# Top-32 threshold of sparse attention: all rows take the search that starts on pairwise larger and smaller halves

## Chip, cores and metric

The kernel runs on one core of a Trainium2 chip. The metric is the device time of one execution in microseconds; the median over several runs counts. The engines are named as in the profile: PE is TensorE, DVE is VectorE, ACT is ScalarE, POOL is GpSimd, SP is SyncE, which here issues most of the transfers.

## The reference

Three layers in a row, all in fp32. The change lies in the first.

```python
scores = scale * np.matmul(q, k.transpose(0, 1, 3, 2))      # 4 x 8 heads, 576 x 576
kth = np.partition(scores, -32, axis=-1)[..., -32:-31]      # the 32nd largest of each row
scores = np.where(scores >= kth, scores, -1e9)
attn = softmax(scores)                                       # exp(scores - max) / sum
x = (attn @ v) reshaped to 2304 x 512
x = ((x @ w_a) * (x @ w_b)) @ w_out                          # 512 -> 1536 -> 512
out = top-1 of 8 experts: gate * (relu(x @ w1[e]) @ w2[e])
```

## The kernel before

The 4 x 8 heads of 576 query rows are cut into 144 tiles of 128 query rows (here called rows of the program). One step of the main loop (line 864) handles one such row on every engine. For row r, PE multiplies and ACT evicts the 128 x 576 scores `s` in two halves (`scores`, lines 364 and 365, two steps ahead). DVE then looks for the 32 largest scores of each query (`topk`, lines 368 to 390) in seven instructions that count: MAX8 writes the eight largest of its input to `t8`, MATCH_REPLACE8 writes the input with these eight set to a very low number, and this repeats until the fourth MAX8 leaves the 32nd largest as its last column. Line 390 turns that into `bi`, a bias for ACT. `softmax` (lines 392 to 402) runs two steps later: ACT makes a penalty for all scores under the threshold (line 397), POOL subtracts it from the scores (line 400, `z<-s,z`), ACT takes the exponential (line 402). PE transposes the result (`turn`, line 419), ACT evicts it (line 422), and `mix` multiplies with v.

Two rows are in work on DVE at a time: lines 904 to 906 take turns between the second half of the row before (`thresholds[0]`) and the first half of the row now (`cur`). The instruction order on PE, DVE, ACT and POOL is fixed by hand; SP's transfers are placed by a scheduler that estimates when they become due. The second layer (lines 639, 652, 683) is fed in pieces into the same steps on PE, ACT and POOL. In the first part of the run weights that come as raw 64-bit words are unpacked as well: two DVE instructions (lines 532 and 534), one on ACT, one on POOL (line 539) and two on PE for each of 36 blocks. The expert layer comes after the attention, from about 880 us on.

`topk` has two forms. The constant FOLD (line 45) is a tuple by which a row picks its form: `FOLD[step % len(FOLD)]` on line 903. With `(0,)` every row takes the plain form: `views = [(t.s, y)] + [(y, y)] * 3`, 576 columns throughout.

Of the kernel before, what the change touches and what calls it, by code (L numbers as in the profile page):

```python
# [41 lines left out]
YB = 2  # L42
XG = 1
RB = 2
FOLD = (0,)
PEN = (0,)
PC = 512
TB = 2
# [34 lines left out]
def fused_kernel(  # L83
# [114 lines left out]
    with ExitStack() as ph:  # L198
# [169 lines left out]
        def topk(t, fold):  # L368


            H2 = S // 2
            t.bi = wk.tile([P, 2], F32, name="bi", bufs=6)
            y = wk.tile([P, S], F32, name="y", bufs=YB)

            t8 = wk.tile([P, 32], F32, name="t8", bufs=6)
            t.top, t.thr = t8[:, 0:1], t8[:, 31:32]
            if fold:
                dve.tensor_tensor(y[:, :H2], t.s[:, :H2], t.s[:, H2:], op=OP.max)
                dve.tensor_tensor(y[:, H2:], t.s[:, :H2], t.s[:, H2:], op=OP.min)
                views = [(y[:, :H2], y[:, :H2])] * 2 + [(y, y)] * 2  # L380
            else:
                views = [(t.s, y)] + [(y, y)] * 3
            for r, (cur, rest) in enumerate(views):
                v = t8[:, r * 8 : r * 8 + 8]
                dve.max(v, cur)  # L385
                yield
                if r < 3:
                    dve.match_replace(out=rest, in_to_replace=v, in_values=cur, imm_value=LOWEST)  # L388
                    yield
            dve.tensor_scalar(t.bi[:, 1:2], t.thr, HUGE, None, op0=OP.mult)  # L390
# [473 lines left out]
        for step in range(-AHEAD_L, NRW + TL + 5):  # L864
# [25 lines left out]
            with tc.high_priority(offset=FG):  # L890
# [11 lines left out]
                if 0 <= step < NRW:  # L902
                    cur = topk(live[step], FOLD[step % len(FOLD)])
                for _ in range(4):
# [404 lines left out]
```

## Time and profile before

| | |
|---|---|
| runs | median 1327.95 us of 3 (1326.23 to 1329.16) |
| profiled execution | 1326.2 us, of which the span from first to last instruction is 1324.5 us |
| PE matmul | 1181.9 us busy, 89% of the span |
| DVE | 913.1 us, 69% |
| ACT | 821.6 us, 62% |
| POOL | 719.9 us, 54% |
| granted TensorE clock, mean | 0.955 |

The shares are averages over unlike stages. Up to about 880 us the 144 rows run and DVE is nearly full; after that DVE has little to do and PE is full. Busy times of one engine do not count overlap of neighbours twice, so a mean duration times a count is a little more than the busy time. A wait is put down to the engine whose signal came last.

### The profile page before, as it was taken

How to read it: one execution, taken by the hardware profiler on the slowest of the kernel's cores; microseconds unless marked ns; L12 is line 12 of the kernel's file. 1: busy time of each engine (PE TensorE's matmuls, PEld its weight loads, DVE VectorE, ACT ScalarE, POOL GpSimd, SP SyncE). 2: the span in 40 equal slices, each digit the busy share in tenths (PEclk: the TensorE clock that was granted, in tenths of full speed). 3: DMA queues.
4: the chain of work that ended last, by engine and by line, in shares of the span. 5: the costliest groups of instructions: out<-in, count | busy, mean ns of one | idle time of the engine just before them, and what ended most of it. 6: DMA issues, size and time to landing. Idle time of an engine off the chain costs nothing. (4 is left out here: it accounts for less than half of the span.)

```text
span 1324.5 us, 23353 instructions
## 1 busy us (share of the span) xinstructions
PE 1181.9 (89%) x7908; PEld 996.1 (75%) x7909; DVE 913.1 (69%) x1995; ACT 821.6 (62%) x1961; POOL 719.9 (54%) x1188
## 2 busy tenths in 40 slices
PE   4766988898999987999998998899999989999996
PEld 3544766677898876888887887677898868888885
DVE  6999999988898986999988898750200135444440
ACT  4777888777777775687777776662532334444441
POOL 4555786766677775767766766564445321111100
PEclk9677999999999997999999998899999989999999
DMA  6334476466695654766765667458988145555520
GB/s 211 118 108 140 159 248 219 164 215 211 202 258 166 187 194 135 209 191 195 194 194 175 204 180 211 135 154 268 324 282 253 32 129 198 174 170 168 177 91 19
DMA packets 129101, 240.56 MB, mean 182 GB/s; under 512 B 24621, under 2 KB 73901, under 8 KB 128978
## 3 DMA queue, kind: packets, MB, share of 16 engines
q1 hardware_dynamic: 124818, 228.74, 55.3%
q0 software_dynamic: 4160, 10.29, 2.4%
q8 instruction: 64, 1.05, 0.3%
q14 instruction: 59, 0.48, 0.1%
HBM read 198.92 MB, written 40.85 MB: 181 GB/s over the span
## 5 line engine op out<-in xcount | busy, mean ns | idle before, releaser
L385 DVE MAX8 t<-y 128x8 f32<-128x576 f32 x432 | 312.0, 750 | 2.9
L400 POOL TENSOR_TENSOR z<-s,z 128x576 f32<-128x576 f32 x144 | 206.0, 1430 | 98.0 <-ACT z L397 95.9
L683 PE MATMUL ab<-xg,wab 128*128 128x256 f32 x1440 | 214.4, 291 | 4.8 <-ACT gab L687 3.1
L388 DVE MATCH_REPLACE8 y<-t,y 128x576 f32<-128x576 f32 x288 | 213.9, 743 | 0.0
L683 PEld LDWEIGHTS ab<-xg,wab 128*128 128x128 f32 x1440 | 189.2, 192 | 8.1 <-ACT gab L687 3.5
L683 PE MATMUL ab<-raw,wab 128*128 128x256 f32 x1152 | 173.4, 292 | 7.2 <-ACT gab L687 4.3
L419 PE MATMUL tr<-ident,z 128*128 128x128 f32 x720 | 137.9, 292 | 41.4 <-ACT z L402 34.7
L683 PEld LDWEIGHTS ab<-raw,wab 128*128 128x128 f32 x1152 | 152.2, 193 | 10.7 <-ACT gab L687 5.0
L402 ACT ACTIVATE z<-z,bi 128x576 f32<-128x576 f32 x144 | 111.4, 774 | 78.2 <-POOL z L400 78.0
L385 DVE MAX8 t<-s 128x8 f32<-128x576 f32 x144 | 107.8, 748 | 59.9 <-ACT s L365 49.0
L364 PE MATMUL tr<-kT,qT 128*128 128x288 f32 x512 | 129.2, 336 | 21.5 <-ACT qT L341 10.9
L422 ACT ACTIVATE wt<-tr 128x384 f32<-128x384 f32 (+2 forms) x320 | 127.3, 412 | 18.5 <-PE tr L419 18.0
L365 ACT ACTIVATE s<-tr 128x288 f32<-128x288 f32 x288 | 118.9, 414 | 30.3 <-PE tr L364 28.7
L652 PE MATMUL x<-wo,gh 128*128 128x512 f32 x432 | 137.7, 400 | 0.0
L419 PEld LDWEIGHTS tr<-ident,z 128*128 128x128 f32 x720 | 92.7, 148 | 56.4 <-ACT z L402 38.8
L1015 DVE TENSOR_TENSOR u<-raw,u 128x1024 fp32r<-128x1024 f32 x64 | 76.3, 1221 | 85.3 <-ACT u L1014 62.5
L639 POOL TENSOR_TENSOR gab<-gab 128x256 f32<-128x256 f32 x108 | 81.5, 754 | 97.0 <-ACT gab L687 92.0
L1064 POOL DMA_INDIRECT out_dram<-o,ids x24 | 23.9, 994 | 201.0 <-ACT o L1063 197.7
L1092 PE MATMUL y<-u,hT 128*128 128x512 f32 (+1 forms) x528 | 128.0, 396 | 0.4 <-DVE hT L1197 0.4
L364 PEld LDWEIGHTS tr<-kT,qT 128*128 128x128 f32 x512 | 90.5, 207 | 37.1 <-ACT qT L341 13.2
L397 ACT ACTIVATE z<-s,bi 128x576 f32<-128x576 f32 x144 | 112.5, 781 | 0.0
L1092 PEld LDWEIGHTS y<-u,hT 128*128 128x128 f32 (+1 forms) x528 | 89.7, 174 | 27.6 <-DVE hT L1197 0.5
(178 smaller groups left out, 2213.8 us busy)
## 6 DMA issues: line engine op xcount, KB each, us to landing
wab<-wab_d SPq DMA_DIRECT2D x192, 512.0 KB, 4.4
raw<-in_moe_w_dram SPq DMA_DIRECT2D x28, 1024.0 KB, 5.1
wab_d<-wab SPq DMA_DIRECT2D x24, 512.0 KB, 3.2
kT<-kT_d SPq DMA_DIRECT2D x20, 576.0 KB, 4.5
vs<-in_v_dram SPq DMA_DIRECT2D x36, 256.0 KB, 3.0
kT_d<-kT SPq DMA_DIRECT2D x16, 576.0 KB, 3.7
raw<-in_moe_w_a_dram SPq DMA_DIRECT2D x12, 512.0 KB, 4.1
raw<-in_moe_w_b_dram SPq DMA_DIRECT2D x12, 512.0 KB, 4.3
```

What stands on the lines that cost most here:

```text
L364: pe.matmul(p, l, r, start=(i == 0), stop=(i == len(terms) - 1))
L365: act.activation(t.s[:, cs], p, AF.Copy, scale=SCALE)
L385: dve.max(v, cur)
L388: dve.match_replace(out=rest, in_to_replace=v, in_values=cur, imm_value=LOWEST)
L397: act.activation(t.w, t.s, AF.Relu, bias=t.bi[:, 1:2], scale=-HUGE)
L400: pool.tensor_tensor(t.w, t.s, t.w, op=OP.subtract)
L402: act.activation(t.w, t.w, AF.Exp, bias=t.bi[:, 0:1], accum_out=t.o.sm[:, t.slot : t.slot + 1])
L419: pe.transpose(pt[:, i * P : (i + 1) * P], t.w[:, k0 : k0 + P], ident)
L422: act.activation(th[:, sl, w], pv[:, :, src], AF.Copy)
L652: pe.matmul(px[t], g[:, ts], wo[:, w, f], start=(f == 0 and i == 0), stop=(f == NF - 1 and i == 2))
L683: pe.matmul(p[:, i], wt[:, a, c, :], xg[x][:, c, :], start=(j == 0), stop=(j == len(terms) - 1))
L1092: pe.matmul(p[:m], (hi, lo)[a], u[:, b, f % 4, :], start=(f == 0 and i == 0), stop=(f == NF2 - 1 and i == 2))
```

## The change

The constant FOLD goes from (0,) to (1,): every row takes the other form of `topk`.

```diff
-FOLD = (0,)
+FOLD = (1,)
```

The lines of `topk` that now run for every row:

```python
dve.tensor_tensor(y[:, :H2], t.s[:, :H2], t.s[:, H2:], op=OP.max)   # H2 = 288
dve.tensor_tensor(y[:, H2:], t.s[:, :H2], t.s[:, H2:], op=OP.min)
views = [(y[:, :H2], y[:, :H2])] * 2 + [(y, y)] * 2
```

Column j of a row is paired with column j + 288; the larger of each pair goes to the left half of `y`, the smaller to the right half. The first 16 largest of the left half are each among the 31 largest of the row, so the first two rounds of MAX8 and MATCH_REPLACE8 search and blank 288 columns only; the last two rounds (MAX8, MATCH_REPLACE8, MAX8) run over all 576. A row has four MAX8 and three MATCH_REPLACE8 as before and two TENSOR_TENSOR more.

On DVE, in the middle of the attention, one step before (number behind `t_` is the row's own buffer; 3952 is the older row, 4011 the newer):

```order
L385 MAX t_3952<-y 128x8
L385 MAX t_4011<-s 128x8
L388 MATCH_REPLACE y<-t_3952,y 128x576
L388 MATCH_REPLACE y<-t_4011,s 128x576
L385 MAX t_3952<-y 128x8
L385 MAX t_4011<-y 128x8
L390 TENSOR_SCALAR bi<-t_3952 128x1
L388 MATCH_REPLACE y<-t_4011,y 128x576
```

And the same step after, where 4050 is the older row and 4111 the newer:

```order
L385 MAX t_4050<-y 128x8
L378 TENSOR_TENSOR y<-s 128x288
L379 TENSOR_TENSOR y<-s 128x288
L385 MAX t_4111<-y 128x8
L388 MATCH_REPLACE y<-t_4050,y 128x576
L388 MATCH_REPLACE y<-t_4111,y 128x288
L385 MAX t_4050<-y 128x8
L385 MAX t_4111<-y 128x8
L390 TENSOR_SCALAR bi<-t_4050 128x1
L388 MATCH_REPLACE y<-t_4111,y 128x288
```

The two TENSOR_TENSOR stand ahead of the newer row's first MAX8, whose place among the others is as it was. The instructions on PE, ACT and POOL and their order are the same in both kernels. On SP three places near the start differ. One of them, a load of k, before:

```order
L241 DMA kr<-in_k_dram 128x2x256
L246 DMA kr<-in_k_dram 64x64 x2
L512 DMA raw_607<-in_moe_w_out_dram 128x1024
L228 DMA qr<-in_q_dram 128x128 x2
L334 DMA kT_d<-kT 128x1152
```

and after:

```order
L241 DMA kr<-in_k_dram 128x2x256
L246 DMA kr<-in_k_dram 64x64
L512 DMA raw_621<-in_moe_w_out_dram 128x1024
L228 DMA qr<-in_q_dram 128x128 x2
L246 DMA kr<-in_k_dram 64x64
L334 DMA kT_d<-kT 128x1152
```

One small load has moved behind three others.

## Rows read from the trace of the kernel before

**Rows 1.** Stages: busy time (and instructions) of each engine, clock, DMA share, GB/s
```profile
33.00:300.00 267.00, 211.59 (x1266) 157.97 (x1265) 249.12 (x541) 209.91 (x476) 174.53 (x231) 0.87 0.52 172
300.00:880.00 580.00, 535.60 (x4040) 460.22 (x4040) 511.79 (x1174) 420.00 (x1110) 398.47 (x706) 0.97 0.64 190
```

**Rows 2.** Instruction groups of DVE, whole span: busy us, mean ns, idle before
```profile
L385 DVE MAX8 t<-y 128x8 f32<-128x576 f32 x432 | 312.0, 750 | 2.9
L388 DVE MATCH_REPLACE8 y<-t,y 128x576 f32<-128x576 f32 x288 | 213.9, 743 | 0.0
...
L1015 DVE TENSOR_TENSOR u<-raw,u 128x1024 fp32r<-128x1024 f32 x64 | 76.3, 1221 | 85.3 <-ACT u L1014 62.5 <-DMA raw<-in_moe_w_dram 22.6
...
L737 DVE MAX8 m<-lg 128x8 f32<-128x8 f32 x18 | 2.9, 163 | 35.1 <-ACT lg L733 35.1
L739 DVE FIND_INDEX8 i<-m,lg 128x8 uint32<-128x8 f32 x18 | 2.9, 160 | 0.0
```

**Rows 3.** Timeline of DVE: start us, us; two MAX8 in a row
```profile
319.41 1.41 DVE L385 MAX8 t<-y 128x8 f32<-128x576 f32 x2
```

**Rows 4.** DVE groups, 33 to 300 us
```profile
L385 DVE MAX8 t<-s 128x8 f32<-128x576 f32 x42 | 31.2, 742 | 4.6 <-ACT s L365 4.6
...
L534 DVE TENSOR_SCALAR w64r<-raw 128x512 int16<-128x512 int16 x33 | 24.6, 745 | 0.0
L532 DVE TENSOR_SCALAR w64t<-raw 128x512 int32<-128x512 int32 x33 | 19.2, 581 | 7.2 <-DMA raw<-in_moe_w_b_dram 5.2 <-DMA raw<-in_moe_w_a_dram 1.9
```

**Rows 5.** Lines 532, 534 and 400 by themselves: shortest/median/longest ns, first and last start
```profile
L532 DVE TENSOR_SCALAR w64t<-raw x36: 405/428/1645, 14.0 to 247.6; 128x512 int32<-128x512 int32 x36
...
L534 DVE TENSOR_SCALAR w64r<-raw x36: 444/462/1709, 14.3 to 248.1; 128x512 int16<-128x512 int16 x36
...
L400 POOL TENSOR_TENSOR z<-s,z x144: 1399/1427/1613, 29.8 to 888.3; 128x576 f32<-128x576 f32 x144
```

**Rows 6.** Timeline of DVE and POOL from 181 us
```profile
181.04 1.57 POOL L400 TENSOR_TENSOR z<-s,z 128x576 f32<-128x576 f32 x1
181.26 1.65 DVE L532 TENSOR_SCALAR w64t<-raw 128x512 int32<-128x512 int32 x1
182.58 1.59 POOL L220 TENSOR_TENSOR ks<-kr,ks 128x576 fp32r<-128x576 f32 x1
182.82 1.66 DVE L534 TENSOR_SCALAR w64r<-raw 128x512 int16<-128x512 int16 x1
```

**Rows 7.** Timeline of DVE and POOL at the start, around a TENSOR_TENSOR of DVE
```profile
10.73 0.40 POOL L218 TENSOR_SCALAR qs<-qr 128x256 fp32r<-128x256 f32 x1 [9.14 <-DMA qr<-in_q_dram]
...
11.21 0.72 POOL L220 TENSOR_TENSOR qs<-qr,qs 128x256 fp32r<-128x256 f32 x1
11.55 1.00 DVE L256 TENSOR_TENSOR ks<-kr,ks 128x576 fp32r<-128x576 f32 x1 [7.94 <-ACT ks L255]
11.91 0.90 POOL L293 TENSOR_SCALAR qs<-qr 128x256 fp32r<-128x256 f32 x1
```

**Rows 8.** Groups of DVE and of ACT, 300 to 880 us
```profile
L385 DVE MAX8 t<-s 128x8 f32<-128x576 f32 x99 | 74.3, 751 | 54.0 <-ACT s L365 43.1 <-ACT lg L733 5.0 <-POOL z L400 2.0
...
L397 ACT ACTIVATE z<-s,bi 128x576 f32<-128x576 f32 x100 | 78.3, 783 | 0.0
```

**Rows 9.** Waits, 300 to 880 us: us in total, times, longest
```profile
ACT z L402 <- POOL z L400: 60.3, 49, 3.4
...
PE tr L364 <- ACT s L365: 8.8, 10, 1.3
...
PE tr L419 <- ACT s L365: 0.9, 1, 0.9
```

**Rows 10.** Waits, 33 to 300 us
```profile
PE tr L419 <- ACT z L402: 29.6, 15, 3.1
...
POOL x1T L539 <- DVE w64r L534: 4.0, 4, 1.7
...
ACT z L402 <- POOL z L400: 12.3, 11, 1.7
```

## The prediction

> **What bounds the kernel now.** I first read the busy time of the engines stage by stage [rows 1]. From 33 to 300 us DVE is busy for 249.1 of 267 us, 93%, while PE has 211.6. From 300 to 880 us PE is first with 535.6 of 580 us, and DVE has 511.8, so 68 us of it are idle. The change touches DVE only, so the two stretches must be priced apart.
>
> Then I read who waits for DVE, and for whom DVE waits. In the late stretch the first MAX8 of a row stands idle for 54.0 us over 99 rows, 43.1 of them for ACT's eviction of the scores, and ACT's first softmax step, which needs DVE's threshold, never stood idle at all: 0.0 over 100 [rows 8]. So there DVE is ahead of the others and starved; a faster DVE would only wait longer. In the early stretch the picture is turned: over 42 rows the first MAX8 waits only 4.6 us [rows 4], DVE has no other room to speak of, and its results are waited for here and there (POOL for the unpacked weights, 4.0 us; PE 29.6 us for ACT's exponential, which is the end of the row's chain) [rows 10]. I take the early stretch to move with DVE, and the late one not.
>
> **What the change removes.** Per row two MAX8 and two MATCH_REPLACE8 go from 576 to 288 columns. MAX8 takes 750 ns over 576 columns and 163 ns over 8 [rows 2], which is 1.033 ns a column, so 288 columns less save 298 ns. MATCH_REPLACE8 shows one width only, 743 ns. FIND_INDEX8, its nearest relative, takes 160 ns over 8 columns [rows 2]; a line from there gives 1.026 ns a column and 296 ns saved. The bounds are no saving and half of 743, 371 ns; I take 296, since an instruction that passes every column once is nearest to its neighbours. Together 2 x 298 + 2 x 296 = 1.19 us a row.
>
> **What it adds.** Two TENSOR_TENSOR of 288 columns. The one form with both inputs in SBUF that is not disturbed takes 1221 ns over 1024 columns [rows 2]; less 736 columns at 1.03 ns leaves 463 ns. Neighbours on DVE overlap: two MAX8 of 750 ns take 1.41 us together [rows 3], so 0.09 us of an instruction lie under the next. The first TENSOR_TENSOR costs 0.37 us for that reason; the second the full 0.46, because the MAX8 behind it reads what it has just written. Together 0.83 us. With nothing else, a row gains 1.19 - 0.83 = 0.36 us.
>
> **The lock.** Something else is there. In the early stretch the unpacking of weights has two neighbouring DVE instructions of about the same length (lines 532 and 534). At their shortest they take 405 and 444 ns, at their longest 1645 and 1709 [rows 5], and the long ones lie against POOL instructions. The clearest place is at 181 us [rows 6]: POOL's subtraction starts at 181.04 and ends at 182.61; DVE's instruction starts at 181.26 and ends at 182.91, a little after POOL's; POOL's next one, begun at 182.58, ends at 184.17; DVE's second, begun at 182.82, ends at 184.48. They take turns, each waiting for the whole of the other's instruction. In the mean the pair took 581 and 745 ns [rows 4], so the waiting cost (581 - 405) + (745 - 444) = 0.48 us a pair while POOL was busy for 174.5 of 267 us [rows 1].
>
> These two have one input each, though, and MAX8 and MATCH_REPLACE8, with one input, show no such lengthening (750 and 743 ns in the mean). What of an instruction with two inputs from SBUF? The trace has one beside a busy POOL, at 11.55 us [rows 7]: 1.00 us for 576 columns, ending 0.62 us after POOL's instruction at 11.93, and that is just 576 columns at 1.03 ns plus a little; POOL's next one took 0.90 us where the same form had taken 0.40 a microsecond earlier. One case, but it speaks both ways for the same taking of turns.
>
> [...]
>
> I take 0.48 us of waiting per pair also for the two TENSOR_TENSOR: POOL's share of time is much the same in both stretches, 65% and 69% [rows 1]. The bounds are 0 (POOL always elsewhere) and the 1.65 + 1.66 - 0.85 = 2.46 us of the place at 181 us. The mean of 33 pairs is the better guide than its worst case. So DVE goes from a gain of 0.36 to a loss of 0.48 - 0.36 = 0.12 us a row.
>
> **The sum on DVE.** Early stretch: 42 rows x 0.12 = 5.0 us longer. Late stretch: 99 x 0.12 = 12 us more on DVE, against 68 us of idle time; nothing shows. If that idle time were gone, the 12 us would count.
>
> **The sum on POOL.** POOL waits as well. Its subtraction (line 400) takes 1427 ns at the median and 1.57 us where it met DVE [rows 5, 6], 0.15 us more; two TENSOR_TENSOR a row make two meetings, 0.3 us a row. POOL is far from full, but ACT waits for just this subtraction, 49 times in the late stretch and 11 times in the early one [rows 9, 10]. 60 x 0.3 = 18 us more waiting on ACT. ACT's own delays reach PE by late evictions: PE's waits for ACT in the late stretch are seven rows from 8.8 down to 0.9 us [rows 9], 31.6 us in all, against 60.3 us of ACT's waiting for POOL. So at most half goes through, 9 us; as PE's waits have other causes too, I take half of that, 4.5 us. The bounds are 0 and 9.
>
> **The rest.** The last part, from 880 us on, has no such rows: 0. SP's three shifts concern small loads a few places later; k and q are fetched ten steps ahead of use, so 0; were that cover gone, one late load of k would cost about a microsecond or two each. PE, ACT and POOL run the same lists.
>
> Sum against the profiled execution: 1326.2 + 5.0 + 4.5 = 1335.7 us. The median of the runs is 1.75 us above that execution, so 1337 us.
>
> **The rivals.**
>
> *The halves win.* If two inputs do not contend, or the pairs fall into POOL's gaps, the gain of 0.36 us stands. It shows in the 42 early rows, 15 us, and not later, where DVE is starved: 1326.2 - 15.1 + 1.75 = 1313 us. [...] It decides at 0.36 us of waiting per pair: below that DVE is faster than before.
>
> *The taking of turns is worse.* A TENSOR_TENSOR that has waited makes POOL's next instruction wait, which then is ready at once when the second comes, as at 181 us. With twice the waiting, 0.96 us, a row costs 0.60 us more: 25 us in the early stretch; in the late stretch 99 x 0.60 = 59 us, still under 68; POOL's whole 9 us come on top: 1326.2 + 34 + 1.75 = 1362 us. A MATCH_REPLACE8 whose time does not shrink with its columns would come out near there as well (0.59 us a row). Beyond 0.69 us a row the late stretch would start to pay too.
>
> *Nothing moves.* DVE's loss is small, and ACT never waited visibly for a threshold; if the early stretch is in truth held by ACT, POOL and PE in turn, and POOL's delay fits in its idle time, the time stays at 1326 to 1330 us.
>
> **How the numbers follow.** About 0.2% (2.7 us) is what a measurement of this kernel can tell from no change. The forecast, a slightly slower kernel, 1328 to 1347 us by its bounds (42 rows at up to 0.24 us, POOL at up to 9 us): 0.44, of which 0.04 lies within 0.2%. The halves win: 0.24. Nothing moves: 0.18. Turns are worse: 0.14. So faster 0.24, same 0.22, slower 0.54. The range runs from 1311 to 1358 us: it takes in the forecast, the rival without movement, half of the first rival and half of the worse one, and leaves out under 0.2.
>
> **What would show it.** In the profile after: MAX8 and MATCH_REPLACE8 over 288 columns at about 452 and 447 ns; TENSOR_TENSOR of lines 378 and 379 at 0.46 us at the shortest and at 0.6 to 0.8 us in the mean, with long ones that end just behind a POOL instruction; line 400 longer than 1427 ns at the median or with many more at 1.6 us; DVE's busy time up by some 10 to 20 us; the idle time before the first instruction of a row still near 50 us in the late stretch. The forecast is wrong if the TENSOR_TENSOR have one steady length, or if the early stretch, 33 to 300 us, comes out shorter.

## The result and the profile after

The changed kernel takes 1335.72 us in the median of 6 runs (1331.09 to 1337.63) against 1327.93 of 6 runs of the kernel before (1325.29 to 1329.16). The ratio is 1.0052 with a 95% interval of 1.0034 to 1.0069, so 7.8 us slower. In later runs it was 1.0044 (1.0026 to 1.0062). The forecast was 1337 us with a range of 1311 to 1358.

The profiled execution of the changed kernel is its fastest run, 1331.1 us, with a span of 1329.3 us. It holds 4.9 us of the loss. Here are the two stretches, to be held against [rows 1]: busy time of PE, PE's weight loads, DVE, ACT and POOL, then clock, DMA share and GB/s.

```profile
33.00:300.00 267.00, 207.22 (x1237) 151.79 (x1237) 250.69 (x616) 206.43 (x470) 182.99 (x227) 0.90 0.50 169
300.00:880.00 580.00, 533.16 (x4034) 458.15 (x4032) 504.37 (x1372) 418.84 (x1109) 416.23 (x701) 0.97 0.63 189
```

In the same 267 us of the early stretch PE and ACT got less far: 1237 matmuls where there were 1266, and 470 instructions on ACT where there were 476. What is longer in both stretches is POOL's busy time, from 174.5 to 183.0 and from 398.5 to 416.2 us; over the whole span it goes from 719.9 to 749.5 us. DVE's is hardly changed: 913.1 before, 910.8 after. The groups of DVE, whole span (busy us, mean ns, idle before), answer to [rows 2]:

```profile
L385 DVE MAX8 t<-y 128x8 f32<-128x576 f32 x288 | 216.5, 752 | 2.9
L385 DVE MAX8 t<-y 128x8 f32<-128x288 f32 x288 | 128.1, 445 | 0.1
L388 DVE MATCH_REPLACE8 y<-t,y 128x288 f32<-128x288 f32 x288 | 127.0, 441 | 0.0
L388 DVE MATCH_REPLACE8 y<-t,y 128x576 f32<-128x576 f32 x144 | 106.4, 739 | 0.0
L378 DVE TENSOR_TENSOR y<-s 128x288 f32<-128x288 f32 x144 | 101.8, 707 | 63.4 <-ACT s L365 62.9
L379 DVE TENSOR_TENSOR y<-s 128x288 f32<-128x288 f32 x144 | 93.9, 652 | 0.0
```

The four shortened searches are as short as they should be. The two TENSOR_TENSOR are not: taken by themselves (shortest, median, longest ns) they run from 0.43 us to 2.8 us.

```profile
L378 DVE TENSOR_TENSOR y<-s x144: 432/510/2846, 18.0 to 877.5; 128x288 f32<-128x288 f32 x144
...
L379 DVE TENSOR_TENSOR y<-s x144: 443/452/1751, 19.0 to 877.9; 128x288 f32<-128x288 f32 x144
```

The timeline of DVE and POOL shows why, in the same manner as [rows 6]:

```profile
185.16 1.29 POOL L539 TENSOR_TENSOR x1T<-w64t,w64r 128x512 int32<-128x512 int32 x1
185.19 1.58 DVE L378 TENSOR_TENSOR y<-s 128x288 f32<-128x288 f32 x1
...
186.42 0.62 POOL L218 TENSOR_SCALAR qs<-qr 128x256 fp32r<-128x256 f32 x1
...
186.69 0.65 DVE L379 TENSOR_TENSOR y<-s 128x288 f32<-128x288 f32 x1
...
187.00 0.41 POOL L399 TENSOR_SCALAR bi<-t 128x1 f32<-128x1 f32 x1
```

DVE's first instruction starts 0.03 us after POOL's and ends at 186.77, 0.32 us after POOL's end at 186.45. POOL's next one, started at 186.42, takes 0.62 us where the same form took 0.40 [rows 7], and DVE's second one then waits for that. POOL's one-column instruction at the end, which has 0.23 us in the mean in the kernel before, has 0.41. They take turns as the unpacking pair does. Not every row meets POOL: counted in this trace, one of the two takes over 0.5 us in 80 of the 144 rows.

### The profile page after: what moved, and what is told of

Same layout as the page of the kernel before. It is cut to its first block, busy times and chain, and to the rows that moved or that the text cites. A ratio compares the mean times of both kernels' runs of the same rounds, so it can differ in the third digit from the quotient of the medians.

```text
span 1329.3 us, 23643 instructions
## 1 busy us (share of the span) xinstructions
PE 1177.3 (89%) x7908; PEld 990.1 (74%) x7909; DVE 910.8 (69%) x2283; ACT 820.1 (62%) x1961; POOL 749.5 (56%) x1188
## 5 line engine op out<-in xcount | busy, mean ns | idle before, releaser
L385 DVE MAX8 t<-y 128x8 f32<-128x576 f32 (+1 forms) x576 | 333.2, 598 | 3.0
L400 POOL TENSOR_TENSOR z<-s,z 128x576 f32<-128x576 f32 x144 | 206.3, 1432 | 83.4 <-ACT z L397 83.1
L388 DVE MATCH_REPLACE8 y<-t,y 128x288 f32<-128x288 f32 (+1 forms) x432 | 231.8, 540 | 0.0
L419 PE MATMUL tr<-ident,z 128*128 128x128 f32 x720 | 135.0, 287 | 43.9 <-ACT z L402 36.6
L364 PE MATMUL tr<-kT,qT 128*128 128x288 f32 x512 | 125.6, 328 | 22.3 <-ACT qT L341 10.9
L378 DVE TENSOR_TENSOR y<-s 128x288 f32<-128x288 f32 x144 | 101.8, 707 | 63.4 <-ACT s L365 62.9
L639 POOL TENSOR_TENSOR gab<-gab 128x256 f32<-128x256 f32 x108 | 84.3, 781 | 90.0 <-ACT gab L687 85.4
L364 PEld LDWEIGHTS tr<-kT,qT 128*128 128x128 f32 x512 | 87.8, 201 | 38.1 <-ACT qT L341 13.2
```

The costliest lines, as they stand in the source:

```text
L364: pe.matmul(p, l, r, start=(i == 0), stop=(i == len(terms) - 1))
L400: pool.tensor_tensor(t.w, t.s, t.w, op=OP.subtract)
L419: pe.transpose(pt[:, i * P : (i + 1) * P], t.w[:, k0 : k0 + P], ident)
```

## Experiments

The theory to be tested: the two TENSOR_TENSOR, with two inputs from SBUF each, and POOL's instructions wait for each other; on DVE that eats what the shorter searches save, and POOL's delay is what the kernel feels. The rivals: SP's changed order of loads (A), DVE in the stretch where it is full (B), something else in the order (C), DVE's results late at a bad moment (D). SP's list, as the traces show it, is that of the kernel before in the run folded late and in the one with DVE slowed, and that of the changed kernel in the run folded early and in the one with ten rows plain. The other kernels have lists of their own.

**The price of the lock, by itself.** Two kernels keep the plain search and add two instructions a row in front of it, whose results are overwritten.

```diff
 (plain form, with two TENSOR_TENSOR added)
+dve.tensor_tensor(y[:, :H2], t.s[:, :H2], t.s[:, H2:], op=OP.max)
+dve.tensor_tensor(y[:, H2:], t.s[:, :H2], t.s[:, H2:], op=OP.min)
 views = [(t.s, y)] + [(y, y)] * 3

 (plain form, with two MAX8 added)
+dve.max(t8[:, 16:24], t.s[:, :H2])
+dve.max(t8[:, 24:32], t.s[:, H2:])
 views = [(t.s, y)] + [(y, y)] * 3
```

> The plain form with the two TENSOR_TENSOR of 288 columns added in front (their result is overwritten). Theory: DVE pays 0.70 us for the pair and 0.5 us of waiting, 1.2 us a row; early stretch 42 x 1.2 = 50 us, late stretch 99 x 1.2 = 119 us against 68 us idle, some of it shows: 1380 to 1430 us; the pair takes 1.2 us and more by its mean durations. Without a lock: as the run with two MAX8 added, within 3 us.

> The plain form with two MAX8 over 288 columns added in front (their result is overwritten). DVE pays 0.7 us a row, no lock: early stretch up to 29 us, late stretch 69 us against 68 us idle: 1345 to 1365 us. The difference to the run with two TENSOR_TENSOR added is the price of the lock: theory 20 us or more; without a lock under 3 us.

Measured: 1410.91 us with the two TENSOR_TENSOR, ratio 1.0634 (1.0596 to 1.0672); 1339.57 us with the two MAX8, 1.0088 (1.0057 to 1.012). The second came out 5 us below what was expected. The stages and the added groups, first of the kernel with TENSOR_TENSOR, then of the one with MAX8:

```profile
300.00:880.00 580.00, 517.76 (x3818) 443.87 (x3817) 576.13 (x1273) 394.65 (x1043) 397.63 (x657) 0.95 0.59 181
...
L383 DVE TENSOR_TENSOR y<-s 128x288 f32<-128x288 f32 x144 | 100.8, 700 | 0.0
L382 DVE TENSOR_TENSOR y<-s 128x288 f32<-128x288 f32 x144 | 100.7, 699 | 1.3 <-ACT s L365 1.3
```

```profile
300.00:880.00 580.00, 532.62 (x4000) 457.46 (x4000) 576.30 (x1366) 419.53 (x1109) 396.07 (x709) 0.97 0.62 188
...
L383 DVE MAX8 t<-s 128x8 f32<-128x288 f32 x144 | 63.9, 444 | 0.0
L382 DVE MAX8 t<-s 128x8 f32<-128x288 f32 x144 | 63.8, 443 | 0.9 <-ACT s L365 0.9
```

In both, DVE is busy for 576 of 580 us, so now it does set the pace. The two kinds of instruction have nearly the same length when undisturbed (TENSOR_TENSOR 432 and 443 ns at the shortest, MAX8 443 and 444 in the mean), yet one pair costs 71.3 us more over 144 rows: 0.50 us a row. That is the lock, read from the time of the whole kernel. DVE's busy time differs by as much (1079.1 against 1007.1 us), and the mean durations say nearly the same: (699 - 432) + (700 - 443) = 0.52 us.

**The changed kernel without the lock.** All rows folded, with two MAX8 in the place of the two TENSOR_TENSOR (the pairing is left out, so the 16th largest score stands where the 32nd should).

```diff
-dve.tensor_tensor(y[:, :H2], t.s[:, :H2], t.s[:, H2:], op=OP.max)
-dve.tensor_tensor(y[:, H2:], t.s[:, :H2], t.s[:, H2:], op=OP.min)
-views = [(y[:, :H2], y[:, :H2])] * 2 + [(y, y)] * 2
+dve.max(t8[:, 16:24], t.s[:, :H2])
+dve.max(t8[:, 24:32], t.s[:, H2:])
+views = [(t.s[:, :H2], y[:, :H2]), (y[:, :H2], y[:, :H2]), (t.s, y), (y, y)]
```

> All rows folded, but the two TENSOR_TENSOR are replaced by two MAX8 over 288 columns, which take about as long by themselves (445 against 432 to 443 ns) and read one input. Left out: the pairing, so that the 16th largest score stands where the 32nd should. Theory: without the second input no lock; the first instructions take a steady 0.45 us, DVE gains 0.5 us a row, POOL is back at its 720 us busy; the early stretch gets shorter, 1312 to 1324 us. Rival C (DVE is not what the early stretch waits for, the loss is something else in the order): DVE's busy time falls by 70 us but the time stays at 1326 to 1330. Rival A: still 1333 to 1337, as SP's list is nearly that of the changed kernel.

Measured: 1325.85 us against 1326.09, ratio 0.9999 (0.9985 to 1.0014). The loss of the changed kernel is gone, as the theory says, but there is no gain in its place, as it does not say. Engines of this run, and its two new instructions:

```profile
PE 1177.0 (89%) x7908; PEld 992.6 (75%) x7909; DVE 842.2 (64%) x2283; ACT 821.8 (62%) x1961; POOL 721.8 (55%) x1188
...
L379 DVE MAX8 t<-s 128x8 f32<-128x288 f32 x144 | 65.0, 451 | 105.8 <-ACT s L365 105.6
L378 DVE MAX8 t<-s 128x8 f32<-128x288 f32 x144 | 64.0, 444 | 4.9 <-ACT s L365 4.8
```

In the kernel before, the first instruction of a row had:

```profile
L385 DVE MAX8 t<-s 128x8 f32<-128x576 f32 x144 | 107.8, 748 | 59.9 <-ACT s L365 49.0 <-ACT lg L733 5.0 <-POOL z L400 2.0
```

DVE is 71 us less busy than before and simply waits longer for the scores: 105.6 us where it waited 49.0. (The first of the two MAX8 reads only the first half of the scores and can start before the second half is there; this lets DVE begin earlier, not later.) So rival C is right on one point: nothing in this kernel gets shorter by a faster DVE, not in the early stretch either. Against rival A it speaks for one of SP's three shifts only, the load of k shown ahead: that one is in this kernel's list too. The other two are not, so this part of the expectation was put too broadly.

**DVE slowed evenly, POOL left alone.** The run above with a third MAX8, over 404 columns, so that DVE loses in each row about what the lock takes.

```diff
 dve.max(t8[:, 24:32], t.s[:, H2:])
+dve.max(t8[:, 8:16], t.s[:, :404])
```

> The run with short searches and two MAX8 instead of the TENSOR_TENSOR (so the 16th largest instead of the 32nd), and one more MAX8 over 404 columns, 0.48 us: DVE loses evenly what the lock takes from it in the mean, POOL is not touched. Theory (the loss goes through POOL): as the kernel before, 1325 to 1328. Rival D (DVE's own waiting): 3 us longer or more, as the changed kernel.

**POOL held up, DVE left fast.** The run without the lock (again the 16th largest) with one small POOL instruction a row behind the subtraction, into a place that nobody reads.

```diff
 pool.tensor_tensor(t.w, t.s, t.w, op=OP.subtract)
+pool.tensor_scalar(t.junk, t.top, -1.0, None, op0=OP.mult)
```

> The same short searches with two MAX8 and no third, and the small POOL instruction behind the subtraction that nobody waits for, 30 us a run: POOL is held up as by the lock, DVE is 70 us less busy than before. Theory: 3 to 6 us longer than the kernel before, although DVE is faster. Rival D: as the kernel before.

Measured: DVE slowed, 1326.58 us, ratio 1.0000 (0.9985 to 1.0015). POOL held up, 1331.08 us, ratio 1.0027 (1.0011 to 1.0044); between the medians it is 5.4 us. The engines, first of the run with DVE slowed, then with POOL held up:

```profile
PE 1179.1 (89%) x7908; PEld 993.3 (75%) x7909; DVE 905.3 (68%) x2427; ACT 821.4 (62%) x1961; POOL 721.7 (54%) x1188
```

```profile
PE 1181.7 (89%) x7908; PEld 996.0 (75%) x7909; DVE 842.1 (63%) x2283; ACT 821.2 (62%) x1961; POOL 747.1 (56%) x1332
```

63 us more on DVE cost nothing; 25 us more on POOL cost 0.27% though DVE is faster than ever. So a delay on POOL of this size is enough for about half of the loss. That the loss goes this way is not shown by it, for two reasons. The slowed DVE is slowed evenly and is no slower than in the kernel before (905.3 against 913.1 us busy), so B and D are tested only in part. And by the order of SP's transfers in the traces the kernel with POOL held up differs from the kernel before in eight places, the one with DVE slowed in none.

**The same on the kernel before, at two places.** The small POOL instruction is added to the plain kernel, once so that ACT's exponential waits for it too (it writes `bi` again), once so that nobody does.

```diff
 pool.tensor_tensor(t.w, t.s, t.w, op=OP.subtract)
+pool.tensor_scalar(t.bi[:, 0:1], t.top, -1.0, None, op0=OP.mult)     (on the chain)
+pool.tensor_scalar(t.junk, t.top, -1.0, None, op0=OP.mult)           (beside it)
```

> The kernel before with one more small POOL instruction a row, right behind the subtraction, on the result that ACT's exponential waits for; DVE as before. It adds about 0.21 us x 144 = 30 us to POOL, what the change added to its busy time (719.9 to 749.5 us), and puts all of it on the row's chain. Theory (the loss goes through POOL's delay): 6 to 12 us longer, 1332 to 1338. Rival D (the loss comes from DVE's results, late at a bad moment by a wait of 1 to 1.6 us): under 3 us.

> As the run before, but the small POOL instruction writes a place that nobody reads, so it only delays what stands behind it on POOL. Theory: less than with the chain, 2 to 8 us longer, 1328 to 1334. Rival D: nothing.

Measured: on the chain 1348.16 us, ratio 1.017 (1.0148 to 1.0192), beyond what was expected; beside it 1330.19 us, 1.0028 (1.0007 to 1.005). Both add 27 to 28 us to POOL; on the chain 22 us of it reach the end, beside it 3.6. So it matters which POOL instruction is late; SP's lists of these two kernels differ from the kernel before as well, in five and in seven places, and what that costs was not tried. In the changed kernel (here first the groups of POOL before, then after) it is not the subtraction, which [rows 5] had at 1427 ns at the median:

```profile
L400 POOL TENSOR_TENSOR z<-s,z 128x576 f32<-128x576 f32 x144 | 206.0, 1430 | 98.0 <-ACT z L397 95.9 <-DMA qr<-in_q_dram 1.6
L639 POOL TENSOR_TENSOR gab<-gab 128x256 f32<-128x256 f32 x108 | 81.5, 754 | 97.0 <-ACT gab L687 92.0 <-PE x L652 2.0 <-ACT lg L733 1.8
...
L399 POOL TENSOR_SCALAR bi<-t 128x1 f32<-128x1 f32 x144 | 33.0, 229 | 0.2
```

```profile
L400 POOL TENSOR_TENSOR z<-s,z 128x576 f32<-128x576 f32 x144 | 206.3, 1432 | 83.4 <-ACT z L397 83.1
...
L639 POOL TENSOR_TENSOR gab<-gab 128x256 f32<-128x256 f32 x108 | 84.3, 781 | 90.0 <-ACT gab L687 85.4 <-ACT lg L733 1.8 <-PE x L652 1.7
...
L399 POOL TENSOR_SCALAR bi<-t 128x1 f32<-128x1 f32 x144 | 40.4, 281 | 0.2
```

The subtraction has 1432 ns in the mean (1430 before). The delay lies on the small instruction ahead of it, 7.4 us over the run, and in bits of 0.3 to 3 us on some twenty other groups. The one ahead of the subtraction seems to be mostly covered: POOL's wait for ACT before the subtraction is shorter by as much and more (95.9 before, 83.1 us after).

**Where in the run.** Folded only late, and only early. SP's list of the first is that of the kernel before, of the second that of the changed kernel.

```diff
-FOLD = (1,)
+FOLD = (0,) * 48 + (1,) * 112      (late)
+FOLD = (1,) * 48 + (0,) * 112      (early)
```

> Plain form in rows 0 to 47, folded in rows 48 to 143. SP's list is then that of the kernel before. Theory (the two TENSOR_TENSOR of a folded row and POOL's instructions wait for each other; that eats what the shorter searches save on DVE, and POOL's delay reaches PE a little): the trace of the changed kernel loses some 2.5 us from row 42 on, so 1329 to 1332 us against 1328. Rival A (the loss comes from SP's changed order of loads): 1328, nothing. Rival B (the loss is all DVE's, in the stretch where DVE is full): 1328, nothing, since DVE is starved in these rows.

> Folded in rows 0 to 47, plain in rows 48 to 143. SP's list is then that of the changed kernel. Theory: 3 to 5 us lost up to row 48, 1331 to 1334 us. Rivals A and B: the whole loss, 1334 to 1337 us.

Measured: late 1328.49 us, ratio 1.0018 (1.0000 to 1.0037); early 1330.63 us, 1.0032 (1.0018 to 1.0047). Together 1.0050, and the whole change has 1.0044 and 1.0052, so the loss looks like two parts that add up. The late part is 2.4 us by the medians, at the edge of what the times can tell from nothing.

The traces say more of it. By the starts of ACT's instructions, each held against the same one in the kernel before, four profiled executions have folded late rows: the late run, the run with ten rows plain (below) and the two profiles of the changed kernel. From 360 to 840 us they fall back by 2.2, 2.2, 2.1 and 2.2 us. The early run and the one with DVE slowed change by -0.3 and 0.1 us there, and the two with the small POOL instruction beside the chain by 0.7 and -0.2. So a late part is there with SP's list as before, in rows where DVE is starved: neither A nor B can be the whole cause. The added POOL instruction makes little or nothing of it.

**One place in the late part.** The largest step of it, first before, then after. The last line of each is the busy time of the engines over 2 us, with the granted clock third from the end:

```profile
495.67 0.19 POOL L769 CAST ds<-st 128x1 int32<-128x1 f32 x1
...
498.40 0.50 PE L652 MATMUL x<-wo,gl 128*128 128x512 f32 x1 [1.90 <-POOL gl L639]
...
498.40:500.40 2.00, 2.00 (x8) 1.53 (x9) 2.00 (x7) 0.97 (x2) 0.23 (x3) 0.80 0.94 189
```

```profile
499.12 0.46 DVE L378 TENSOR_TENSOR y<-s 128x288 f32<-128x288 f32 x1 [1.03 <-ACT s L365]
...
499.21 0.42 POOL L769 CAST ds<-st 128x1 int32<-128x1 f32 x1
...
502.17 0.79 PE L652 MATMUL x<-wo,gl 128*128 128x512 f32 x1 [2.13 <-POOL gl L639]
...
502.20:504.20 2.00, 2.00 (x5) 1.61 (x6) 1.65 (x6) 0.35 (x1) 0.20 (x2) 0.50 1.00 342
```

POOL's CAST meets DVE's TENSOR_TENSOR and takes 0.42 us instead of 0.19. PE, which waits for a result that POOL makes behind it, waits 2.13 us instead of 1.90, and over the 2 us after that wait the granted clock is 0.50 where it was 0.80. By 510 us this execution is 1.3 us further behind. The CAST takes 418 to 420 ns in all four executions with folded late rows and 183 to 192 in the nine others; the 1.3 us are in three of the four, and in the late run 0.8 us are lost and made up again. Here the lock reaches PE through POOL.

**One place in the early part.** In the profile of the changed kernel the steps of each row keep 1.5 us ahead of the kernel before until 183 us and are 2.8 us behind it at 200. Granted clock (the third number from the end) and engines from 190 to 200 us, first before, then after:

```profile
190.00:200.00 10.00, 8.41 (x58) 5.45 (x57) 10.00 (x21) 8.12 (x20) 7.53 (x9) 1.00 0.79 266
```

```profile
190.00:200.00 10.00, 8.21 (x39) 4.81 (x39) 10.00 (x28) 5.47 (x13) 4.65 (x5) 0.66 0.63 223
```

And the timeline after, just ahead of it:

```profile
183.08 1.55 DVE L534 TENSOR_SCALAR w64r<-raw 128x512 int16<-128x512 int16 x1
...
184.70 0.38 SPq L512 DMA_DIRECT2D raw<-in_moe_w_a_dram  x1
...
189.35 0.78 ACT L535 ACTIVATE w64r<-raw 128x512 int16<-128x512 uint32 x1 [1.32 <-DMA raw<-in_moe_w_a_dram]
...
191.79 0.80 PE L551 MATMUL tr<-wab,minusr 128*128 128x512 f32 x1 [3.07 <-ACT wab L547]
```

An unpacking instruction of DVE, held up by POOL, frees a weight buffer; SP loads the next weights at 184.70; ACT waits 1.32 us for them, PE 3.07 us for ACT; and from 190 to 200 us, with the end of this idle time in them, PE is granted a clock of 0.66 where it had 1.00, and does 39 matmuls where it did 58. The kernel before, at the same place:

```profile
184.55 0.38 SPq L512 DMA_DIRECT2D raw<-in_moe_w_a_dram  x1
...
188.76 1.41 ACT L535 ACTIVATE w64r<-raw 128x512 int16<-128x512 uint32 x2
...
191.82 0.50 PE L551 MATMUL tr<-wab,minusr 128*128 128x512 f32 x1 [1.59 <-ACT wab L547]
```

There the unpacking instruction was held up by POOL as well [rows 6], and the load went out at nearly the same time, but ACT came to it 1.4 us later and did not wait. After the change the other engines are that much ahead and DVE, with the waits in its own instructions, is not. So here it is DVE's result that comes late for the others: rival D, at this one place. In the second profile of the changed kernel ACT waits for the same load and the place costs 2.7 us. In the early run it costs 4.5 us, after a wait of the same ACT instruction that the profile puts down to POOL. In the run with these rows plain, the late run, the run without the lock and the one with DVE slowed it costs at most 0.4 us. A part can be made up later (1.6 of the 4.3 us by 250 us in the first profile). To see whether the folded rows around this place are the early loss, ten of them were left plain.

```diff
-FOLD = (1,)
+FOLD = (1,) * 22 + (0,) * 10 + (1,) * 128
```

> Folded in all rows but 22 to 31, which DVE works on around 160 to 225 us, where the trace of the changed kernel loses 4.4 us (PE's clock at 0.66 from 190 to 200 us, in the kernel before at 1.0). SP's list is that of the changed kernel. If the early loss is that one place: 3 to 4.5 us less than the changed kernel. If it is spread over all folded rows: about 10/48 of the early loss less, under 1 us.

> The changed kernel again, to have it on the same chip and in the same rounds as the others: 1.003 to 1.007 of the kernel before. The theories do not differ here.

Measured side by side: 1330.18 us, ratio 1.0020 (1.0005 to 1.0035), with ten rows plain; 1332.18 us, 1.0044 (1.0026 to 1.0062), with all folded. 2.0 us less by the medians, between the two answers. The two intervals overlap, but both are taken against the kernel before; held against each other, the means are 1330.1 us of 12 runs and 1332.6 of 8, 2.5 us apart with a standard error of 0.9. SP's list is the same in both. So these ten folded rows cost time by themselves, and A is not the whole cause of the early part. The profile of the first has the clock at 1.0 at this place and loses nothing there, but had lost 2.8 us before it, so the place is not the whole early loss either.

## Why the prediction was right, step by step

The time, the sign and the size came out: +9.5 us by the sum, +7.8 measured. The lock, on which the sign hung, was right. Inside DVE's term two errors nearly cancelled, which is luck, and POOL's term was worked out at a place where nothing changed. The range of 1311 to 1358 us would have held "nothing moves" too, so that it was kept says little by itself.

- *What the shorter searches save*: 305 and 302 ns each against 298 and 296 forecast. Right.
- *What the TENSOR_TENSOR cost alone*: 432 and 443 ns against 463, and the second overlaps its successor like the first (from 199.50 to 199.95 us, with the MAX8 starting at 199.87); where POOL is elsewhere, the pair takes 0.73 us from start to start, as in the timeline of DVE below, and the sum had 0.83. The gain without a lock is thus 1.21 - 0.73 = 0.48 us a row and not 0.36.

```profile
199.14 0.44 DVE L378 TENSOR_TENSOR y<-s 128x288 f32<-128x288 f32 x1
199.50 0.45 DVE L379 TENSOR_TENSOR y<-s 128x288 f32<-128x288 f32 x1
199.87 0.45 DVE L385 MAX8 t<-y 128x8 f32<-128x288 f32 x1
```

- *The lock on DVE*: (707 - 432) + (652 - 443) = 0.48 us a row in the mean, as the 0.48 taken from the unpacking pair. That the two agree so closely is chance: single waits run up to 2.4 us, and only 80 of 144 rows show a long one. The step from a pair with one input each to one with two, which hung on a single instruction of the trace, holds: the two kernels with added instructions differ by 0.50 us a row, and the timeline shows the turns at 185 us. Why the two engines take turns, no run shows.
- *DVE's balance*: over the whole run 0.48 us a row gained and 0.48 lost; DVE's busy time should have risen by 10 to 20 us and fell by 2.3. But the sum took its 0.12 us a row from the early rows, and there, from 33 to 300 us, the pair waits longer than later (the second two lines, 300 to 880 us):

```profile
L378 DVE TENSOR_TENSOR y<-s 128x288 f32<-128x288 f32 x42 | 33.8, 806 | 0.1
...
L379 DVE TENSOR_TENSOR y<-s 128x288 f32<-128x288 f32 x42 | 29.8, 710 | 0.0
...
L378 DVE TENSOR_TENSOR y<-s 128x288 f32<-128x288 f32 x99 | 64.8, 654 | 61.9 <-ACT s L365 61.5
L379 DVE TENSOR_TENSOR y<-s 128x288 f32<-128x288 f32 x99 | 62.4, 630 | 0.0
```

  That is (806 - 432) + (710 - 443) = 0.64 us, a loss of 0.16 us a row; the second profile of the changed kernel and that of the early run give 0.11 and 0.02. In the late stretch the waiting is 0.41 us, which leaves a small gain that nobody waits for. The TENSOR_TENSOR's own cost was put 0.1 us too high and the lock in the early rows up to 0.16 too low. So the term of 5.0 us came out near for reasons that cancel: the run folded only early lost 4.5 us, POOL's part in it included.
- *"I take the early stretch to move with DVE"*: wrong towards faster. Without the lock DVE works 71 us less and nothing gets shorter. The signs were in the rows and beside them: ACT's threshold step never idled before DVE, in the early stretch neither (below), and the first MAX8 waited little there because the scores had been ready for 8.4 us in the median, against 0.4 us in the late stretch.

```profile
L397 ACT ACTIVATE z<-s,bi 128x576 f32<-128x576 f32 x41 | 31.9, 779 | 0.0
```

  A busy engine that nobody waits for is not the bound. It becomes one when it gets slower: with two MAX8 more a row, 94 us of DVE, the kernel loses 14 us, and its profile is some 12 us behind by row 42.
- *DVE starved in the late stretch*: right; the idle time before the first instruction of a row goes from 54.0 us [rows 8] to 61.9 us.
- *POOL's term*: 4.5 us, bounds 0 and 9. The size is of the right order (3.6 to 3.7 us by the ratios for 25 to 27 us of delay on POOL in two runs, SP's shifts in them included), the place is wrong. It was worked out from a longer subtraction and ACT's longer wait for it, and neither is there: the line below, from 300 to 880 us after, has 60.6 us where [rows 9] had 60.3.

```profile
ACT z L402 <- POOL z L400: 60.6, 49, 3.5
```

  The delay lies on other POOL instructions, such as the CAST at 499 us. Beside the chain about an eighth of a delay was passed on in these runs. On the chain it was 22 of 28 us, far more than the "at most half" of the sum, so a subtraction made 0.3 us longer in every row, as forecast, would have cost much more than 4.5 us. No run shows the "two meetings" a row behind that 0.3 us either: 64 of the 144 rows have no long TENSOR_TENSOR, and the subtraction has 1432 ns in the mean where it had 1430.
- *The rivals*: "the halves win" fell with the lock, and would have fallen without it, as the run without the lock shows. "Nothing moves" was right that a faster DVE changes nothing.
- *SP's three shifts at 0*: shown for the load of k, open for the other two. The one or two microseconds named for a late load of k were a guess and stand in no run; the run without the lock, with that shift in its list, took 1325.85 us against 1326.09.

What stays open: two places were followed to PE, one through DVE's late result at 183 us and one through POOL's at 499 us. How the whole loss divides between these two ways, what made the 2.8 us before 160 us in the run with ten rows plain, and what SP's two other shifts cost was not settled. POOL's delay as imitated costs 0.27% or 0.28%, the change 0.44% to 0.52%, but the imitation loses its time at other places and under other lists of SP, so it does not measure POOL's share. No version that was run beats the kernel before; with a gain of nothing even for short searches without a lock, I expect none from shorter searches alone.

## What to carry to other kernels

Before an instruction is made cheaper, look for someone who waits for its result: 93% busy is no proof. Price a TENSOR_TENSOR with two SBUF inputs on DVE, beside a POOL as busy as here (65% and 69%), with the time that POOL holds it up, stretch by stretch, and take that from a neighbouring pair in the trace that already meets POOL; here it was 0.48 us a row in the mean, as large as the whole saving, and 0.64 in the stretch that counted. And count what the other engine loses by it: an engine at 55% can be on the chain of every step, where 0.23 us a row cost 22 us, or beside it, where as much cost 3.6. When an imitated delay costs about as much as the change, see in the traces whether it does so at the same places.

## What the hardware showed that was not expected

The waiting of either engine lies inside the instruction's duration and counts as busy, not as idle: the TENSOR_TENSOR at 185.19 us has 1.58 us where the shortest has 0.43. So DVE shows 69% after as before, though (0.275 + 0.209) x 144 = 70 us of it are now waiting, and only the shortest duration beside the mean gives it away. It also hits POOL instructions of a single column: the one on line 399 went from 229 to 281 ns in the mean. And a second input is not the only way into it: the unpacking pair, with one input each, waits in both kernels (at the longest 1645 and 1709 ns before [rows 5, 6], 1476 and 1706 after).
